# Second half of the key weights loaded ahead of the third pair of x tiles, with the orders of the head rebuilt around it

## The chip, the cores and the metric

The kernel runs on one core of a Trainium2 chip. The metric is the device time of one execution in microseconds (us); a figure for a kernel is the median of its executions. Times inside one execution count from the start of its span.

The engines are named as in the profile: PE is the tensor engine, ACT is ScalarE, DVE is VectorE, POOL is GpSimd, and SP is the engine that issues most loads.

## The reference

One transformer layer on 2048 tokens of width 448, with 16 heads of width 28: a linear attention with softmax features, then a gated unit of width 1792. Only the attention's first steps matter here.

```python
xn  = layernorm(x)                                  # over the 448 columns
q, k, v = split(xn @ wqkv)                          # 16 heads of 28
phi_k = concat(softmax(k @ w_phi), softmax(-(k @ w_phi)))   # per head
kv = einsum("bhsf,bhsd->bhfd", phi_k, v)            # summed over all tokens
...                                                 # the same features for q, division, wo
h  = x + attention
h2 = h + (sigmoid(hn @ w_gate) * (hn @ w_up)) @ w_down,   hn = layernorm(h)
```

## The kernel before

The kernel is a list of named operations, each with what it reads and writes, and one string of names for each engine that fixes the order in which that engine runs them. Waits follow from the data and the orders. The change edits these strings and hardly anything else, so the names are needed.

- The 16 tiles of x have 128 tokens each. `x1` and `x0` are loads of one tile (112 KB); `x2`, `x4` and so on are loads of a pair (224 KB), so `x2` brings tiles 2 and 3; it is the third load of x, and the texts call it the third x pair. `ld_k0` and `ld_k2` are the two halves of the key weights (196 KB each).
- `bst`, `agg`: statistics of a tile, on DVE. `ve1`, `pow1`, `nm1`, `nb1`: the scale and shift that follow from them, nearly all on POOL. `xn`: the normalized tile. `xT`: its transpose, with the copy `xTe`.
- `wT0` to `wT3` transpose the key weights on PE, `wTe` copy them out, `w2m0` multiply them by `w_phi`, and `w2e0` evict the product Wk. One product with Wk then gives k @ w_phi directly.
- `ppa0 ppb0` project tiles 0 and 1 on Wk, `vva0 vvb0` give their values; `ppa2` and the rest do the same for tiles 2 and 3. `ek` is the pair of exponentials, `ss` and `rs` the sums and reciprocals, `phi` the multiply that completes the softmax features, and `kva kvb` the product with the values.
- `warm0` to `warm9` are dummy products of zeros that keep PE busy.

The heads of the five orders, as far as the argument goes:

```python
"sp":   "x1 x0 ld_k0 x2 ld_k2 x4 x6 ld_v0 x10 ld_v2 x8 ld_q2 ld_q1 ld_q0 x12 ..."
"act":  "wphi3 wphi2 wphi1 wphi0 wTe0 wTe1 xT1e xT0e wTe2 w2e0_0 w2e0_1 w2e0_2 w2e0_3 xn3 xn4 ek0 ek1 xn5 ..."
"pe":   "warm0 warm1 warm2 wT0 wT1 xT1 warm3 xT0 warm4 warm5 wT2 w2m0_0 wT3 warm6 w2m0_1 w2m0_2 warm7 w2m0_3
         warm8 ppa0 warm9 ppb0 vva0 xT3 xT2 vvb0 ppa2 ppb2 vva2 vvb2 ..."
"dve":  "zero bd0 bst1 agg1 ve1_1 bst0 agg0 nm1_0 xn1 xn0 bst2 agg2 bst3 agg3 bst4 bst5 wTe3 agg4 agg5 bst6 ..."
"pool": "neghalf ident0 ident phipad wqpad mask0 nm1_1 pow1_1 ve1_0 pow1_0 nm1_2 mask1 ve1_2 ve1_3 pow1_3 nm1_3
         pow1_2 nb1_3 ve1_4 nm1_4 pow1_4 nb1_4 nb1_2 xn2 mask2 opad0 ve1_6 pow1_6 ve1_8 v1ones pow1_8 nb1_6 phi0
         nb1_8 xn7 phi1 phi2 phi3 ... phi8 phi9 phi11 phi12 phi13 phi14 ..."
```

The scales are worked out in groups of tiles; each group costs one `pow` on POOL, whatever its size:

```python
def rstd(ts):                       # a, b: first tile and last tile + 1; n = b - a
    ...
    op("pool", "pow1_%d" % a, lambda e: e.tensor_tensor(rst1[:, a:b], ve1[:, a:b], neghalf[:, 0:n], ALU.pow), ...)
    ...
for ts in ([0], [1], [2], [3], [4, 5], [6, 7], [8, 9, 10, 11], [12, 13, 14, 15]):
    ...
    rstd(ts)
```

And the dummies, each with its count and width:

```python
for i, (n, size) in enumerate(((9, 512), (1, 128), (1, 128), (2, 128), (1, 128), (8, 128), (4, 128), (7, 128), (9, 128), (2, 128))):
    op("pe", "warm%d" % i, warm(n, size), r=["zero"], w=[B(3)])
```

The softmax here doesn't subtract the row's maximum and nothing guards it: scores larger than these inputs give would overflow.

## Time and profile before

| of the kernel before | value |
|---|---|
| time, median of 3 runs | 205.57 us (205.4 to 205.91) |
| span of the profiled execution | 203.7 us |
| PE busy | 97% of the span |
| third x pair issued, landed | 2.17, 5.33 us |
| second half of the keys issued, landed | 2.67, 6.30 us |
| DVE turns to tile 2's statistics | 6.17 us |
| first key projection ppa0 | 10.18 us |
| first exponential ek0 | 12.12 us |
| second key projection ppa2 | 14.02 us |

A line of the timeline gives start, duration, engine, source line, operation, output and inputs with their sizes and a count; a bracket at its end holds the idle time before it and what ended that.

### The profile page before, as it was taken

Reading aid. Unit: us, or ns where it says so; the run is one execution under the profiler, and the core shown is the slowest. Engines: PE = TensorE matmul, PEld = TensorE weight load, DVE = VectorE, ACT = ScalarE, POOL = GpSimd, SP = SyncE. Lnnn points to the kernel's source line nnn. Section 1 sums busy time; section 2 is a strip of 40 time slices with the busy share of each in tenths; the row PEclk is TensorE's granted clock in tenths of the full one; section 3 lists DMA queues with packets and bytes.
Section 4 is the critical chain, followed back from the end, with each engine's and each line's share of the span. In section 5 each row is a group of like instructions: output and inputs, shape, how many; then the busy total and the mean of one; then the engine's idle time right before and its main releaser. Section 6 shows DMA issues by size and latency. Waiting matters only on the chain.

```text
span 203.7 us, 5834 instructions
## 1 busy us (share of the span) xinstructions
PE 196.7 (97%) x2474; PEld 111.6 (55%) x2474; DVE 135.9 (67%) x340; ACT 97.4 (48%) x195; POOL 57.9 (28%) x98
## 2 busy tenths in 40 slices
PE   7899999999979999999999999999999999999995
PEld 3744556655448876777444544444555555554443
DVE  5899999978799988677668967526532422262224
ACT  2889999889892544522333343323522222222220
POOL 4699999942345310400023020001400000000000
PEclk9999999999999999999999999999999999999999
DMA  6975633899522371240004511040212000004002
GB/s 163 306 139 122 77 73 66 282 295 352 141 52 55 55 100 27 55 81 0 3 0 80 119 30 28 2 77 24 56 36 60 3 0 3 0 0 138 0 0 90
DMA packets 32866, 16.25 MB, mean 80 GB/s; under 512 B 25096, under 2 KB 31944, under 8 KB 32840
## 3 DMA queue, kind: packets, MB, share of 16 engines
q1 hardware_dynamic: 32336, 15.86, 33.2%
q8 instruction: 19, 0.31, 0.7%
q10 hardware_dynamic: 504, 0.03, 0.2%
q14 instruction: 7, 0.06, 0.1%
HBM read 8.34 MB, written 1.84 MB: 50 GB/s over the span
## 4 chain that ended last, share of the span: by engine, by line
PE 89%; DVE 4%; ACT 3%; DMA 1%; issue 1%; POOL 0%; DVEq 0%
PE psum L296 82%; PE psum L852 5%; DVE st L499 2%; DMA x_sb<-in_A_x_dram 1%; ACT eq L653 1%; ACT eq L652 1%; PE psum L567 1%; ACT junk L756 1%; ACT x_sb L748 1%; PE psum L492 1%; DVE kvz L683 1%; DVE mv L500 0%; DVE b_sb L717 0%; DVE c_sb L720 0%; POOL rst L512 0%
## 5 line engine op out<-in xcount | busy, mean ns | idle before, releaser
L296 PE MATMUL psum<-xnT,wg_sb 64*128 64x512 bf16 (+1 forms) x490 | 93.3, 333 | 0.4 <-ACT eq L653 0.2
L296 PE MATMUL psum<-xnT,wu_sb 64*128 64x512 bf16 (+1 forms) x490 | 93.0, 333 | 0.0
L824 ACT ACTIVATE sg_sb<-psum 128x512 bf16<-128x512 f32 (+1 forms) x70 | 35.0, 512 | 89.6 <-PE psum L296 89.0
L825 DVE SCALAR_TENSOR_TENSOR hhT<-sg_sb,psum 128x512 bf16<-128x512 bf16 (+1 forms) x70 | 39.0, 577 | 52.5 <-ACT sg_sb L824 52.1
L296 PEld LDWEIGHTS psum<-xnT,wg_sb 64*128 64x128 bf16 x490 | 44.3, 94 | 22.9 <-DVE hhT L825 4.8
L296 PEld LDWEIGHTS psum<-xnT,wu_sb 64*128 64x128 bf16 x490 | 44.3, 94 | 13.0
L296 PE MATMUL psum<-wd_sb,hhT 64*128 64x448 bf16 x336 | 36.9, 349 | 0.0
L296 PEld LDWEIGHTS psum<-wd_sb,hhT 64*128 64x128 bf16 x336 | 17.3, 94 | 14.8 <-DVE x_sb L751 0.6
L622 POOL TENSOR_TENSOR phi<-hhT,rs 128x896 bf16<-128x896 bf16 x14 | 24.1, 1738 | 0.9 <-PE psum L296 0.8
L296 PE MATMUL psum<-Wk,xnT 64*128 64x448 bf16 x112 | 22.3, 350 | 0.2
L296 PE MATMUL psum<-wv_sb,xnT 64*128 64x448 bf16 x112 | 22.4, 351 | 0.1
L759 POOL TENSOR_SCALAR ve<-ssq 128x1 f32<-128x1 f32 x16 | 3.1, 192 | 66.1 <-ACT junk L756 65.7
L618 DVE TENSOR_REDUCE ss<-hhT 128x32 f32<-128x896 bf16 x16 | 17.0, 1062 | 0.7 <-ACT hhT L615 0.7
L296 PE MATMUL psum<-xnT,Wq 64*120 64x512 bf16 x112 | 15.0, 385 | 0.1
L729 POOL TENSOR_TENSOR o_pad<-c_sb,rden 128x448 bf16<-128x448 bf16 x10 | 9.3, 936 | 15.6 <-DVE rden L725 13.4
L296 PE MATMUL psum<-wo_o,oT 64*128 64x448 bf16 x56 | 13.2, 350 | 0.0
L296 PE MATMUL psum<-wo_e,oT 64*128 64x448 bf16 x56 | 13.1, 349 | 0.0
L756 ACT ACTIVATE junk<-x_sb,nm 128x448 bf16<-128x448 bf16 x16 | 10.6, 661 | 1.9 <-DVE nm L754 1.8
L852 PE MATMUL psum<-wd_sb,hhT 128*128 128x448 bf16 (+2 forms) x70 | 11.1, 316 | 0.0
L859 DVE SCALAR_TENSOR_TENSOR x_sb<-psum,x_sb 128x448 bf16<-128x448 f32 (+2 forms) x17 | 9.4, 591 | 2.1 <-PE psum L852 1.6
L499 DVE BATCH_NORM_STATS2 st<-x_sb 128x6 f32<-128x448 bf16 x16 | 9.4, 611 | 1.9 <-DMA x_sb<-in_A_x_dram 1.9
L296 PEld LDWEIGHTS psum<-Wk,xnT 64*128 64x128 bf16 x112 | 7.6, 94 | 5.3 <-ACT hhT L615 0.7
(87 smaller groups left out, 240.3 us busy)
## 6 DMA issues: line engine op xcount, KB each, us to landing
out_dram<-x_sb SPq DMA_DIRECT2D x15, 112.0 KB, 1.8
x_sb<-in_A_x_dram SPq DMA_DIRECT2D x7, 224.0 KB, 4.5
wd_sb<-in_B_w_down_dram SPq DMA_DIRECT2D x7, 224.0 KB, 9.3
wg_sb<-in_B_w_gate_dram SPq DMA_DIRECT2D x3, 448.0 KB, 8.2
wu_sb<-in_B_w_up_dram SPq DMA_DIRECT2D x3, 448.0 KB, 6.9
wv_sb<-in_A_wqkv_dram SPq DMA_DIRECT2D x2, 224.0 KB, 5.0
wk_sb<-in_A_wqkv_dram SPq DMA_DIRECT2D x2, 196.0 KB, 3.3
wo_e<-in_A_wo_dram SPq DMA_DIRECT2D x1, 336.0 KB, 7.9
```

The lines of the kernel that those rows point to most:

```text
L296: p = e.matmul(o, lhsT=w, rhs=r, start=st, stop=sp, tile_position=(row, 0))
L492: p = e.transpose(ps[:, kt * P:(kt + 1) * P], src, ident[:])
L499: op("dve", "bst%d" % t, lambda e: e.bn_stats(st1[:, t, :], x_sb[:, t, :]), r=[("x", t)], w=[("st1", t)])
L618: op("dve", "ss%d" % t, lambda e: e.tensor_reduce(ss[:, s, :], eks, AX.X, ALU.add), r=[("ek", s)], w=[("ss", s)])
L622: return e.tensor_tensor(phi[:, sp, :, :, :].rearrange("p b a n -> p (b a) n")[:, :, 0:56].rearrange("p b (h d) -> p b h d", h=2), eks.rea ...
L729: return e.tensor_tensor(o_pad[:, t % NO, off:off + D].rearrange("p (h d) -> p h d", h=H), c_sb[:, t % NS, :, 0:DH], rden[:, t % NS, :][:, ...
L756: op("act", "sq%d" % t, lambda e: e.activation(junk[:, t % 2, :], h_sb[:, t, :], ACT.Square, bias=nm2[:, t:t + 1], accum_out=ssq2[:, t:t + ...
L759: op("pool", "ve%d" % t, lambda e: e.tensor_scalar(ve2[:, t:t + 1], ssq2[:, t:t + 1], 1.0 / D, EPS, op0=ALU.mult, op1=ALU.add), r=[("ssq2" ...
L824: op("act", "sig" + nm, lambda e: e.activation(sg_sb[:, k, 0:N], bk(bg)[:, 0:N], ACT.Tanh, scale=0.5), r=[B(bg)], w=[("sg", k)])
L825: op("dve", "hh" + nm, lambda e: e.scalar_tensor_tensor(out=hhT[(t0 // 4) % NHH][:, ff, ns], in0=sg_sb[:, k, 0:N], scalar=1.0, in1=bk(bu)[ ...
L852: p = e.matmul(bk(b)[:, lo:hi], lhsT=hb[:, ff, TS(t)], rhs=wd_sb[:, ff, lo:hi], start=ff == 0, stop=ff == FT - 1)
L859: op("dve", "fin%d%s" % (t, nm), lambda e: e.scalar_tensor_tensor(out=h_sb[:, t, lo:hi], in0=bk(b)[:, lo:hi], scalar=0.5, in1=h_sb[:, t, l ...
```

## The change

Its intent was to load by need. The trace shows that the second keys land late (6.30 us) and that their copy wTe3 stands behind the statistics of tiles 4 and 5 on DVE. So the keys go ahead of the third x pair, and what uses them moves up on PE, ACT and DVE. POOL gets small setup steps into its waits, and three dummies go.

```diff
 sp:   x1 x0 ld_k0
-      x2 ld_k2 x4 ...  ld_q1 ld_q0 x12
+      ld_k2 x2 x4 ...  ld_q1 x12 ld_q0
 act:  wTe0 wTe1
-      xT1e xT0e wTe2 w2e0_0 ...  xn5 v1_0 v1_1
+      xT0e wTe2 xT1e w2e0_0 ...  xn5 v1_1 v1_0
 pe:
-      warm0 warm1 warm2 wT0 wT1 xT1 warm3 xT0 warm4 warm5 wT2 w2m0_0 wT3 ... ppa0 warm9 ppb0 vva0 xT3 xT2 vvb0
+      warm0 warm1 wT0 wT1 xT1 warm2 wT2 warm3 xT0 warm4 w2m0_0 wT3 ...       ppa0 warm9 xT3 ppb0 vva0 xT2 vvb0
 dve:  bst2 agg2 bst3 agg3
-      bst4 bst5 wTe3 agg4 agg5
+      wTe3 bst5 bst4 agg5 agg4                 # and small exchanges among bst7 ... agg13
 pool:
-      ident phipad ... nm1_2 mask1 ve1_2 ve1_3 ... nb1_2 xn2 mask2 opad0 ... ve1_8 v1ones pow1_8 ... phi1 phi2 phi3
+      phipad ident ... nm1_2 ve1_2 mask1 ve1_3 ... nb1_2 v1ones xn2 opad0 ... ve1_8 pow1_8 ... phi1 phi2 mask2 phi3
 dummies:
-      (9,512) 1 1 2 1 8 4 7 9 2
+      (8,512) 2 1 1 2 4 4 4 14 1               # the small ones have 128 columns
```

## The prediction

> **What bounds the kernel now.** I read the page first, for the busy shares, then the chain of waits, then the timeline of each engine over the first 20 us, because the change rewrites only orders that belong there.
>
> ```profile
> span 203.7 us, 5834 instructions
> PE 196.7 (97%) x2474; PEld 111.6 (55%) x2474; DVE 135.9 (67%) x340; ACT 97.4 (48%) x195; POOL 57.9 (28%) x98
> PE 89%; DVE 4%; ACT 3%; DMA 1%; issue 1%; POOL 0%; DVEq 0%
> ```
>
> The tensor engine (PE) is busy 97% of the span and carries 89% of the chain. Real matmuls stand nearly without a gap from about 10 us to the end: in a table by stage PE is busy 6.00 of 6.00 us from 18 to 24, from 24 to 30 and from 30 to 36, and 7.99 of 8.00 from 36 to 44. The change removes no real matmul. It can gain only by letting this block start earlier. The chain of waits (start, duration, what) shows what stands before it:
>
> ```profile
> 5.84 0.41 DVE xn_pad L528
> 6.25 0.55 DVE st L499
> 6.80 0.02 issue
> 6.82 0.18 DVE mv L500
> 7.00 0.52 DVE st L499
> 7.53 0.02 issue
> 7.55 0.18 DVE mv L500
> 7.73 1.10 DVE st L499 x2
> 8.84 0.30 DVE WkT L485
> 9.14 0.05 issue
> 9.18 0.39 PE psum L567 x4
> 9.57 0.02 issue
> 9.59 0.54 ACT Wk L485
> 10.13 0.05 issue
> 10.18 0.93 PE psum L296 x8
> ```
>
> VectorE (DVE) takes the statistics of x tiles 2 and 3, then of 4 and 5 (the x2 of 1.10 us), and only then copies the last transposed key block, WkT (wTe3). The fold into Wk (w2m0_3), its eviction by ScalarE (ACT) and the first key projection (ppa0, at 10.18) follow. So at first sight the two statistics cost ppa0 about 1.1 us, and moving wTe3 ahead of them looks like the gain. But a second chain runs beside it, on GpSimd (POOL) and ACT, and it is nearly as late:
>
> ```profile
> 10.31 0.72 POOL L512 TENSOR_TENSOR rst<-ve,neghalf 128x2 f32<-128x2 f32 x1
> 11.17 0.34 POOL L516 TENSOR_TENSOR nb<-nm,rst 128x2 f32<-128x2 f32 x2
> 11.40 0.81 ACT L525 ACTIVATE xn_pad<-x_sb,nb,rst 128x512 bf16<-128x512 bf16 x1 [0.57 <-POOL nb L516]
> 12.12 0.52 ACT L614 ACTIVATE hhT<-psum 128x448 bf16<-128x448 f32 x1
> ```
>
> ACT idles 0.57 us for nb of tiles 4 and 5, normalizes tile 4 (xn4), and only then takes the first exponential ek0, at 12.12. From there it runs ek0, ek1 with no gap until 13.94; ppa2 needs ek1's bank and starts at 14.02. PE's own work (ppa0, ppb0, vva0, two transposes, vvb0) ends at 13.98. **Two chains meet at 14.0 us**, and both must shorten for the packed block to move.
>
> **What the Trainium skill says.** "Perfetto Trace Analysis", section "Tensor Engine Instruction (MATMUL, LD_WEIGHTS)": ACT, DVE and GpSimd are strict FIFO. The trace agrees: ek0's input (ppb0) was done at 12.00, yet ek0 began only at 12.12, as xn4 before it in the queue was running out. "DMA: Bandwidth & Descriptors", section "Issuing engines are not separate DMA queues": all transfers share the same 16 DMA engines and interleave. Here the sum of a transfer's issue and its time to landing gives x1 2.9, x0 3.9, first keys 4.8, third x pair (x2) 5.4, second keys 6.3, x4 7.6 us: in issue order, so exchanging two neighbours should trade their places, not speed both. "TensorE: Matmul & The Clock Gate", section "What's actually happening": the array starts at half clock and is released after some 3.4 us of activity. The trace agrees in kind: the weight loads of the first 512-column dummies are 0.43 us apart until 3.77 and then speed up, some 2.6 us after the first matmul.
>
> **The change part by part.**
> 1. Loads exchanged. Second keys (196 KB) took 6.3 - 5.4 = 0.9 us of the queue, x2 (224 KB) 5.4 - 4.8 = 0.57 us. After: keys at 4.8 + 0.9 = 5.7, x2 at 5.7 + 0.57 = 6.27. DVE started tile 2's statistics at 6.17, right behind xn0. So x2 now lands 0.1 us too late: statistics of 2 and 3 end (agg3) at about 7.83 in place of 7.73. **Cost 0.1 us, on the second chain.**
> 2. Transposes of the second keys. wT2 ran at 7.05, behind ten dummies and xT0, although its data were there at 6.3. Now it runs at 5.75, ahead of xT0 (6.31, which waits for xn0). But ACT takes xT0e first: it can start at 6.75, when xT0 is done, and ACT idles there 0.5 us that xT1e filled before. Then at the trace's pitches: wTe2 7.25, xT1e 7.65, and the four evictions from 8.15, 0.44 apart, so the fourth ends at 8.15 + 3 x 0.44 + 0.53 = 10.0. Before it ended at 10.12.
> 3. wTe3 before the statistics of 4 and 5: at about 7.9 in place of 8.75, and w2m0_3 at about 8.3 in place of 9.18. ACT is then the limit, so of that 0.85 us only the **0.12 us** of step 2 reaches ppa0, now at about 10.05.
> 4. Dummies. 9 to 8 of 512 columns; the 34 or so small ones (1+1+2+1+8+4+7+9+2 = 35) become 33. Small ones take some 60 to 75 ns each. The large one removed frees PE at about 4.4 in place of 4.8, but wT0 waits for the first keys until 4.80 anyway: nothing gained. In the stretch after ppa0 two become one: under 0.1 us.
> 5. xT3 before ppb0: ppb0 slides by half of the 0.62 us that the two transposes took, so its end stays near 12.0. ek0 still waits for xn4, so this costs nothing.
> 6. POOL. One mask select (0.33 us) leaves the stretch before phi0, another moves one place. nb of tile 4 still follows two of the 0.57 us powers, one of 0.72 us and five small operations; it is bound by agg3. Its mask now fills the wait for agg3, which gives back about half of step 1's 0.1 us. phi0 may start 0.2 us earlier, but its first reader (kva0, 17.96) was not waiting: phi0 ended at 17.23.
> 7. x12 issued ahead of one query transpose: it lands some 1.3 us sooner, and its statistics (16.1) were not waiting. Nothing.
>
> Sum: first chain (ppa0 to vvb0) about 0.12 + 0.1 = 0.2 us shorter; second chain (agg3, nb, xn4, ek1) 0.05 to 0.1 us longer. The later one wins at 14 us: the packed block starts 0 to 0.1 us later. Time 205.57 + 0.05, less a little for repeats in which the clock is released later and the ninth large dummy would have held up wT0: I take **205.5 us**.
>
> **Rivals.**
> A. The head really shortens by the 0.85 us that wTe3 gains. For: the chain of waits puts exactly this stretch on the path. Against: the 0.57 us ACT wait for POOL and the 0.02 to 0.1 us by which both chains miss each other at 14.0. It would give 204.7.
> B. x2 lands later than worked out, at 6.6 or more, because landings vary (3.1 to 3.6 us for the same key size): everything from agg3 on slips by the excess, one for one. It would give 205.9 to 206.2.
> C. The second keys are not sooner: wT2 now stands ahead of xT0 in PE's queue and would hold up xT0, xT0e and all that ACT does after it. Landing at 6.3 would push the fourth eviction to about 10.4 and ek0 to 12.4: about 205.9.
> D. PE cools for want of dummies. PE had 8.10 busy of the first 10 us, and about three dummies in all go; the idle before wT0 grows to 0.4 us. I think it stays warm; if not, small matmuls at half speed until 10 us would cost about 1 us.
>
> **Range and chances.** The whole affair lies in some 4 us of head, and 2% is 4.1 us, so only an accident leaves the band: faster 0.01, same 0.98, slower 0.01. The three runs of before spread 0.5 us. A gives the lower and B and C the upper side: **204.9 to 206.2**.
>
> **What would show it.** Step 1: DVE waits for x_sb by about 0.1 us ahead of tile 2's statistics, near 6.3. Step 2: ACT idles about 0.5 us before its first xnT copy, and the last Wk eviction ends near 10.0. Step 3: the WkT copy on DVE stands near 7.9 and PE no longer waits for it. The core of it: xn4 still begins after an ACT wait for POOL's nb, at 11.4 to 11.5, and ppa2 at about 14.0 to 14.1. If ppa2 stands before 13.7 the second chain was not the bound and A was right; if agg3 stands after 8.0, B was. The rest of the program, from 18 us on, should be the old one, moved by the same amount; a difference arising there would make my reasoning wrong altogether.

## The result, and the profile after

| | before | changed | difference |
|---|---|---|---|
| median | 205.57 us | 205.73 us | |
| range | 205.4 to 205.91 (3 runs) | 205.44 to 205.9 (4 runs) | |
| ratio, 95% interval | | 1.0009 (0.9987 to 1.003): the same | |
| third x pair landed | 5.33 | 6.87 | +1.54 |
| second keys landed | 6.30 | 5.43 | -0.87 |
| copy wTe3 | 8.75 | 8.38 | -0.37 |
| ppa0 | 10.18 | 9.99 | -0.19 |
| xn4 | 11.40 | 12.12 | +0.72 |
| ppa2 | 14.02 | 14.72 | +0.70 |
| DVE's last addition, behind the last product | 201.41 | 201.67 | +0.26 |

A ratio is the mean time of one kernel's fast runs over that of the other's of the same rounds, so not quite the ratio of the medians. Four runs of before took part in it (median 205.49 us). A second measurement of the changed kernel (e6 below) gave 1.003 (1.0005 to 1.0056): slower by a few tenths of a per cent at most. So the first measurement alone shows no loss; what follows about the head is read from traces, one execution each.

The page of the changed kernel, its span, busy times and the chain of waits by engine:

```profile
span 204.0 us, 5831 instructions
PE 196.1 (96%) x2471; PEld 111.0 (54%) x2471; DVE 135.0 (66%) x340; ACT 97.0 (48%) x195; POOL 57.4 (28%) x98
PE 86%; ACT 4%; DVE 2%; DMA 2%; POOL 2%; issue 1%; SPq 1%; POOLq 0%
```

POOL's share of the chain has gone from 0 to 2% and that of PE from 89 to 86%: another chain now leads into the packed block. The chain of waits names it (start, duration, what):

```profile
2.67 4.21 DMA x_sb<-in_A_x_dram
...
8.88 0.57 POOL rst L512
...
11.08 0.69 POOL rst L512
...
14.72 0.95 PE psum L296 x8
```

It starts at the load of the third x pair, 4.21 us from issue to landing, and runs over DVE's statistics, POOL's powers, ACT's normalization and the exponentials to ppa2. Nothing of the key weights is left in it. First, from the timelines of the kernel before, the moments at which DVE takes tile 2's statistics and PE takes ppa2:

```profile
6.17 0.62 DVE L499 BATCH_NORM_STATS2 st<-x_sb 128x6 f32<-128x448 bf16 x1
14.02 1.73 PE L296 MATMUL psum<-Wk,xnT 64*128 64x448 bf16 x14
```

Then the changed kernel's timelines of DVE, ACT and PE (the DVE and ACT lines at 6.90 and 12.12 are links of the chain above too), with the idle time before each in brackets:

```profile
6.90 0.63 DVE L499 BATCH_NORM_STATS2 st<-x_sb 128x6 f32<-128x448 bf16 x1 [0.70 <-DMA x_sb<-in_A_x_dram]
8.38 0.36 DVE L485 COPY WkT<-psum 112x448 bf16<-112x448 bf16 x1
9.99 0.93 PE L296 MATMUL psum<-Wk,xnT 64*128 64x448 bf16 x8
12.12 0.81 ACT L525 ACTIVATE xn_pad<-x_sb,nb,rst 128x512 bf16<-128x512 bf16 x1 [0.82 <-POOL nb L516]
14.72 1.74 PE L296 MATMUL psum<-Wk,xnT 64*128 64x448 bf16 x14 [0.48 <-ACT hhT L615]
```

DVE now stands 0.70 us waiting for x. The first chain did improve: ppa0 starts 0.19 us sooner. But ACT waits 0.82 us for POOL's nb in place of 0.57, takes xn4 0.72 us later, and PE waits 0.48 us for ACT's exponentials ahead of ppa2.

So the head lost 0.7 us, yet the program lost only 0.26. The shift of the same instruction between the two traces shows where the rest went: +0.70 at ppa2, +0.57 from vva2 on (before had small waits there which the longer wait swallowed), still +0.57 at 43 us, then +0.38 until 112 us, and +0.26 from there to the end. The step at 43 us is sharp. PE's timeline of before around it, the 16 key-value products of tiles 13 and 14 (v,phi) and the query projections behind them:

```profile
42.94 0.58 PE L296 MATMUL psum<-v,phi 64*128 64x58 bf16 x16
43.36 0.84 PE L296 MATMUL psum<-xnT,Wq 64*120 64x512 bf16 x6
```

And of the changed kernel:

```profile
43.51 0.39 PE L296 MATMUL psum<-v,phi 64*128 64x58 bf16 x16
43.74 0.85 PE L296 MATMUL psum<-xnT,Wq 64*120 64x512 bf16 x6
```

From the start of the 16 products to the next group takes 43.36 - 42.94 = 0.42 us before and 43.74 - 43.51 = 0.23 us after. In the old kernel the second eight wait for tile 14's features, which POOL finishes at 43.18. In the changed kernel they don't wait. That is 0.19 us given back, and POOL's timeline of before tells why it was late there. These are the multiplies of tiles 9 and 11 (tile 10's is DVE's):

```profile
34.00 1.70 POOL L622 TENSOR_TENSOR phi<-hhT,rs 128x896 bf16<-128x896 bf16 x1 [0.39 <-PE psum L296]
36.11 2.09 POOL L622 TENSOR_TENSOR phi<-hhT,rs 128x896 bf16<-128x896 bf16 x1 [0.41 <-PE psum L296]
```

In the changed kernel, tiles 8 and 9 run back to back:

```profile
32.63 3.36 POOL L622 TENSOR_TENSOR phi<-hhT,rs 128x896 bf16<-128x896 bf16 x2
```

POOL idled 0.39 us ahead of tile 9 before, and doesn't after. The bracket puts this down to PE, but what POOL waits for there had been reached by 33.63 us. "Perfetto Trace Analysis", section "GPSIMD Engine Instruction", of the Trainium skill advises timing POOL by the spacing of starts rather than by reported durations; that spacing agrees: tiles 8 and 9 start 34.00 - 31.91 = 2.09 us apart before and 34.28 - 32.63 = 1.65 us after.

### The profile page after: what moved, and what is told of

Read it like the earlier page. It is cut to its first block, busy times and chain, and to the rows that moved or that the text cites. A ratio compares the mean times of both kernels' runs of the same rounds, so it can differ in the third digit from the quotient of the medians.

```text
span 204.0 us, 5831 instructions
## 1 busy us (share of the span) xinstructions
PE 196.1 (96%) x2471; PEld 111.0 (54%) x2471; DVE 135.0 (66%) x340; ACT 97.0 (48%) x195; POOL 57.4 (28%) x98
## 4 chain that ended last, share of the span: by engine, by line
PE 86%; ACT 4%; DVE 2%; DMA 2%; POOL 2%; issue 1%; SPq 1%; POOLq 0%
PE psum L296 80%; PE psum L852 5%; DMA x_sb<-in_A_x_dram 2%; ACT eq L653 1%; ACT eq L652 1%; SPq L395 1%; POOL rst L512 1%; ACT junk L756 1%; ACT x_sb L748 1%; DVE kvz L683 1%; PE psum L567 0%; ACT hhT L615 0%; ACT hhT L614 0%; ACT xn_pad L525 0%; POOL nm L510 0%
## 5 line engine op out<-in xcount | busy, mean ns | idle before, releaser
L622 POOL TENSOR_TENSOR phi<-hhT,rs 128x896 bf16<-128x896 bf16 x14 | 23.6, 1712 | 1.0 <-PE psum L296 1.0
```

Of the source, the lines that this page charges most:

```text
L622: return e.tensor_tensor(phi[:, sp, :, :, :].rearrange("p b a n -> p (b a) n")[:, :, 0:56].rearrange("p b (h d) -> p b h d", h=2), eks.rea ...
```

## The experiments

The theory after the result: two chains meet ahead of ppa2, and the later one sets the block. The first goes through the keys and ppa0; the second through the third x pair, POOL's powers and xn4. The change helps the first and costs the second. The first rival is that the head doesn't matter, because the change lies inside the noise. The second is that it is not the loads but the new orders on POOL or PE that cost. Each run was correct. A profile is of one execution, and it is not always a typical one: those of e1, e2, e3, e5 and e9 were the slowest of their runs, those of e6, e8 and e11 the fastest. e1 to e4 shared one chip, e5 to e8 a second, e9 to e11 a third, and e12 had a fourth.

### e1: the changed kernel with the loads in their old order

```diff
- sp: x1 x0 ld_k0 ld_k2 x2 x4     (changed kernel)
+ sp: x1 x0 ld_k0 x2 ld_k2 x4
```

> The changed kernel with one thing undone: the third x tile pair (x2) is loaded ahead of the second key half again. My theory, that the exchange of the two loads alone made tile 2's statistics 0.7 us late: x2 lands near 5.3 again, agg3 ends near 7.8 in place of 8.47, tile 4's normalization starts at 11.4 to 11.5 in place of 12.12, and ppa2 at 14.0 to 14.3 in place of 14.72; the time falls back to that of the kernel before (ratio 0.999 to 1.001). The rival, that the new orders of ACT, POOL and PE cause the delay: ppa2 stays at 14.6 or later and the ratio near 1.001 to 1.002.

Measured: 205.45 us, ratio 1.0006 (0.9992 to 1.0019). The third x pair landed at 5.79 and DVE took it without a wait, at 6.08; xn4 followed xn3 with no wait for POOL, as the theory has it. But ppa2 stood at 14.55, not at 14.0 to 14.3, and just short of the rival's 14.6. PE's and ACT's timelines say why (ppa0, then ek0):

```profile
10.62 0.93 PE L296 MATMUL psum<-Wk,xnT 64*128 64x448 bf16 x8 [0.45 <-ACT Wk L485]
12.65 0.54 ACT L614 ACTIVATE hhT<-psum 128x448 bf16<-128x448 f32 x1 [0.53 <-PE psum L296]
```

Now the first chain is the later one. The second keys landed at 6.54, wT2 ran at 6.59 and held up xT0 behind it (6.90), and ppa0 slipped to 10.62. The new orders need the early keys: without them they cost something too, which the second rival has right, but on the first chain and not on POOL. The prediction's rival C, which was wrong for the changed kernel itself, is seen here. The time does not show this cost: it is that of before, while the profiled execution took 206.05 us, and its block lost another 0.53 us between 24.8 and 26.8 us.

### e2: the kernel before with the exchange of loads alone

```diff
- sp: x1 x0 ld_k0 x2 ld_k2 x4     (kernel before)
+ sp: x1 x0 ld_k0 ld_k2 x2 x4
```

> The kernel before with only the two loads exchanged. My theory: x2 lands near 6.9, agg3 ends near 8.45, the key copy of DVE comes behind the statistics of 4 and 5 and so near 9.6, the first key projection near 11.0 and ppa2 at 14.7 to 14.9; the packed block moves by 0.6 to 0.8 us, the span by 0.3 to 0.5 us (part of it given back near 43 us). The rival, that the loads are hidden and the new orders cost it: ppa2 stays near 14.0 and the time that of before.

Measured: 205.93 us, ratio 1.0025 (1.0013 to 1.0038). The exchange alone costs, and the interval leaves out 1, so the first rival, noise, falls for the exchange: a small loss is there. For the changed kernel as a whole it falls only by e6's interval. In DVE's and PE's timelines:

```profile
7.19 0.63 DVE L499 BATCH_NORM_STATS2 st<-x_sb 128x6 f32<-128x448 bf16 x1 [1.01 <-DMA x_sb<-in_A_x_dram]
15.02 1.74 PE L296 MATMUL psum<-Wk,xnT 64*128 64x448 bf16 x14
```

The pair landed at 7.17. DVE waited 1.01 us, and ppa2 came 1.00 us later than in the profile of before, a little more than expected. The copy wTe3, still behind four statistics, slipped too, to 9.72. POOL's gap ahead of tile 9 is still there (0.39 us), and nothing was given back there, against the expectation: the shift is +0.99 at 44 us.

### e3: the kernel before with the copy wTe3 moved ahead of tiles 4 and 5

```diff
- dve: ... agg3 bst4 bst5 wTe3 agg4 agg5
+ dve: ... agg3 wTe3 bst4 bst5 agg4 agg5
```

> The kernel before with only the last key copy of DVE moved ahead of the statistics of tiles 4 and 5. Two-chains theory (the prediction's): the first key projection moves from 10.18 to about 9.9, but tile 4's normalization still waits for POOL until 11.4 and ek0 starts at 12.1, so ppa2 stays at 13.95 to 14.05 and the time is that of before within 0.1 us. The rival, that the chain of waits shown by the profile is the only one: ppa2 at 13.7 and 0.3 us off the time.

Measured: 205.67 us, ratio 1.0013 (1.0 to 1.0026). No gain: what the chain of waits of before seemed to promise (1.1 us of statistics ahead of the copy) is not there. The profile is not a clean one, though. PE's clock was released later in it (its dummies' weight loads were 0.43 us apart until 5.05 us), wT0 stood behind the dummies until 5.26, and the copy waited for PE. ppa0 stood at 10.21 and ppa2 at 14.36, both later than expected. What ppa2 waited for last was neither chain, but DVE's copies of the transposed tiles 2 and 3 (0.35 us), which came late as well. So this run shows that the copy alone gains nothing, but its trace doesn't show by how much the second chain hides it.

### e4: e3 with one power for tiles 2 and 3 on POOL

```diff
  dve as in e3
- for ts in ([0], [1], [2], [3], [4, 5], ...
+ for ts in ([0], [1], [2, 3], [4, 5], ...
- pool: pow1_0 nm1_2 mask1 ve1_2 ve1_3 pow1_3 nm1_3 pow1_2 nb1_3 ve1_4 nm1_4 pow1_4 nb1_4 nb1_2 xn2
+ pool: pow1_0 mask1 ve1_2 nm1_2 pow1_2 nb1_2 ve1_4 nm1_4 pow1_4 nb1_4 xn2
```

> As the run with the copy first, and the second chain shortened too: tiles 2 and 3 share their scale computation on POOL (one power of two columns in place of two of one), so that the nb of tile 4 comes near 10.5 in place of 11.36. Two-chains theory: now both are shorter, ek0 starts near 11.8, ppa2 at 13.6 to 13.8, and the block up to 43 us moves by 0.2 to 0.4 us; of that 0.1 to 0.3 us reach the end of the span (ratio 0.9985 to 0.9995). If something else holds ek0 or ppa2: no change against before.

Measured: 204.92 us, ratio 0.9982 (0.997 to 0.9994): faster by 0.2%. This shortens both chains. xn4 and ppa2:

```profile
11.12 0.81 ACT L525 ACTIVATE xn_pad<-x_sb,nb,rst 128x512 bf16<-128x512 bf16 x1 [0.47 <-POOL nb L516]
14.00 1.73 PE L296 MATMUL psum<-Wk,xnT 64*128 64x448 bf16 x14 [0.21 <-DVE xnT L485]
```

xn4 starts 0.28 us sooner than before, and the exponentials end at 13.70. ppa2 gains only 0.02, and not the 0.2 to 0.4 expected, for it now waits 0.21 us for DVE's copies of the transposed tiles 2 and 3, a third chain. The products behind it lost their small waits: the shift is -0.23 from there on and -0.44 at 44 us, where POOL's gap ahead of tile 9 is gone as well. So about half of the gain up to there is the head's, and the other half is the gap's (below).

### e5: the kernel before with the joint power alone

```diff
  dve as before; groups and pool as in e4
```

> The kernel before with only the joint power of tiles 2 and 3, the other half of the faster version. Two-chains theory: nb of tile 4 near 10.6, tile 4's normalization right behind tile 3's, no longer waiting for POOL; but the key copy still stands behind the statistics of 4 and 5, the first key projection stays near 10.2 and PE's own work ends near 14.0, so ppa2 stays at 13.9 to 14.1: ratio 0.999 to 1.000, clearly less gain than with both. The rival, that the gain of the faster version is all POOL's: ratio near 0.998.

Measured: 205.03 us, ratio 0.9983 (0.997 to 0.9996). It was expected to gain less than e4 and it gained as much, so the rival is right here: the gain of e4 comes with the edit of POOL, and the copy adds nothing that these runs can measure. How much of it is the shorter chain and how much the lost gap, the times don't tell. The profiled execution was the slowest of the five (205.79 us; tiles 4 and 5 landed at 8.14 and DVE waited 0.47 us for them), so its head can't be compared. Past the head it shows what e4 shows: no gap ahead of tile 9, and a shift that goes from +0.27 to +0.06 at 44 us.

### e6: the changed kernel once more

No edit.

> The changed kernel once more, for a second trace and a narrower interval. If the lateness of x2 belongs to the change and not to one execution, it lands at 6.6 to 7.2 again and ppa2 stands at 14.5 to 15.0; ratio 1.000 to 1.002.

Measured: 205.57 us, ratio 1.003 (1.0005 to 1.0056) over six runs; two of them, 206.22 and 207.31 (at a clock of 0.992), lift the mean. In the profiled execution, the fastest, the third x pair landed at 6.54 and ppa2 stood at 14.38, both a little earlier than expected. The loss of the head is thus 0.36 us here and 0.70 us in the first profile; it varies with the landing of the pair. The shift falls from +0.24 to +0.02 at 44 us, so the step of about 0.2 us repeats.

### e7: the changed kernel with the small loads of w_phi behind the x tiles

The four loads of w_phi have rows of 56 bytes and run at the same time, issued by ACT.

```diff
- act: wphi3 wphi2 wphi1 wphi0 wTe0 ...                       (changed kernel)
+ act: wTe0 ...
- sp:  x1 x0 ld_k0 ld_k2 x2 x4 x6 ld_v0 ...
+ sp:  x1 x0 ld_k0 ld_k2 x2 x4 x6 wphi3 wphi2 wphi1 wphi0 ld_v0 ...
```

> The changed kernel with the four loads of the small feature weights (56-byte rows) taken off ACT's queue and issued behind x6 on the sync engine's. They then come too late for the fold, so the time means nothing; the reading is x2's landing. If the small rows in flight from 2.5 to 6.5 us hold up x2 (sharing the same 16 engines), it lands at 6.3 or earlier in place of 6.87 and 7.17. If it is only x2's new place behind the second keys, it stays at 6.7 or later.

Measured: one run, 206.59 us, of unknown state. The third x pair landed at 6.44, between the two expectations: inconclusive on the small rows. Together with the other profiles it helps to settle the main point, though. Here are the landings in all fourteen profiles, those of before and of the changed kernel among them (median and range, us):

| | fourth load in the queue | fifth load in the queue |
|---|---|---|
| old order, 9 profiles | x pair, 5.80 (5.33 to 6.12) | second keys, 6.62 (6.15 to 7.09) |
| new order, 5 profiles | second keys, 5.54 (5.37 to 5.72) | x pair, 6.56 (6.44 to 7.17) |

The fifth load lands at the same time whichever it is. Both orders have moved the same bytes by then, so the place in the queue decides, not the tensor.

### e8: the changed kernel with the joint power

```diff
  changed kernel; groups as in e4
- pool: pow1_0 nm1_2 ve1_2 mask1 ve1_3 pow1_3 nm1_3 pow1_2 nb1_3 ve1_4 nm1_4 pow1_4 nb1_4 nb1_2 v1ones xn2
+ pool: pow1_0 mask1 ve1_2 nm1_2 pow1_2 nb1_2 ve1_4 nm1_4 pow1_4 nb1_4 v1ones xn2
```

> The changed kernel with the second chain shortened by the same joint power. If what the change loses is lost on that chain (statistics of 2 and 3, POOL, tile 4's normalization, ek0), then nb of tile 4 comes 0.4 to 0.7 us sooner than in the changed kernel, ek0 at 12.2 to 12.5, ppa2 at 14.0 to 14.3 in place of 14.72, and the time falls to 0.998 to 1.000 of before. If the chain of keys and PE is what it loses on: ppa2 stays at 14.6 and the ratio near 1.001.

Measured: 205.37 us, ratio 1.0 (0.9988 to 1.0011). ppa2 in PE's timeline:

```profile
14.11 1.74 PE L296 MATMUL psum<-Wk,xnT 64*128 64x448 bf16 x14 [0.19 <-ACT hhT L615]
```

The x pair landed at 6.56, as in e6 (6.54), and ppa2 came 0.27 us sooner than in e6, xn4 0.33 us sooner. Nothing of the first chain was touched: ppa0 stood at 10.17, and at 10.12 in e6. So in the changed kernel the second chain is the bound, which is the theory's core; both kernels lack POOL's gap, so that plays no part. The time is that of before again, though the intervals of e8 and e6 overlap a little.

### e9 and e10: what removes POOL's gap ahead of tile 9

e9 moves one of the setup steps back behind the third features, as the change does; e10 splits the first memset into three parts that write the same columns, for two more instructions at the very start of POOL's stream, where POOL has time.

```diff
e9:   (kernel before)
- pool: ... xn2 mask2 opad0 ... phi1 phi2 phi3
+ pool: ... xn2 opad0 ... phi1 phi2 mask2 phi3
e10:  (kernel before)
- op("pool", "neghalf", lambda e: e.memset(neghalf[:], -0.5), w=["neghalf"])
+ op("pool", "neghalf", lambda e: [e.memset(neghalf[:, i:i + 1 + (i == 2)], -0.5) for i in range(3)][-1], w=["neghalf"])
```

> The kernel before with one POOL instruction moved, as the change moves it: the second mask select from before phi0 to behind phi2. POOL of the kernel before stands idle for 0.39 us ahead of its tenth phi (tile 9, at 34.00), although the semaphores it waited for had come by 33.63; the changed kernel has no such gap, and its packed block gets 0.21 us back at 43 us, where kva14 waits for phi14. If the order of POOL is what removes the gap, then here too: phi14 ends near 42.8 in place of 43.18, kva15 0.2 us sooner, ratio 0.999. If the gap depends on where the instruction stands in POOL's stream (the moved one still stands ahead of tile 9): it stays at 0.35 to 0.4, and the time is that of before.

> The kernel before with two more instructions on POOL that cost nothing: the memset of the constant -0.5 is split in three, at 0.8 us, where POOL has slack until 3.8. Everything behind them stands two places later in POOL's stream. If the gap ahead of tile 9's phi belongs to a place in the stream, it is gone (or at another phi), phi14 ends near 42.8, and the time is 0.999 of before. If it belongs to what POOL waits for: it stays, and the time too.

Measured: e9 205.27 us, ratio 0.9989 (0.9968 to 1.0009); e10 205.33 us, ratio 0.9992 (0.9974 to 1.0009). Neither time differs from before. In the traces e9 keeps the gap (0.40 us) and e10 loses it. Tiles 8 and 9 on POOL in e10, then the 16 products on PE and what follows them:

```profile
32.16 3.44 POOL L622 TENSOR_TENSOR phi<-hhT,rs 128x896 bf16<-128x896 bf16 x2
43.19 0.39 PE L296 MATMUL psum<-v,phi 64*128 64x58 bf16 x16
43.42 0.85 PE L296 MATMUL psum<-xnT,Wq 64*120 64x512 bf16 x6
```

e10's head was 0.25 us late in this profile (the load x0 landed late), and the shift fell to +0.03 at 44 us. The 16 products take 43.42 - 43.19 = 0.23 us to the next group, as in the changed kernel. Two memsets that compute nothing new thus give back the same 0.2 us as the change did.

Counting POOL's records (instructions and waits) that start before tile 9's multiply gives the pattern over all kernels:

| records before tile 9 | kernels | gap, us |
|---|---|---|
| 68 | before, e2, e3, e9 | 0.37 to 0.40 |
| 65 | e4, e5, e11, e12 | 0 to 0.04 |
| 67 | e8 | 0 |
| 70 | changed, e1, e6, e7, e10 | 0 to 0.04 |

So the gap belongs to a place in POOL's stream, and shifting the stream puts another record there. In the kernels with 70, that record is tile 8's multiply, and it shows no gap. But there a delay would be hidden: in the changed kernel its waits were over 0.72 us before tile 7's multiply ended (at 31.95 and 32.67 us), whereas in the kernel before those of tile 9's were over only 0.06 us before tile 8's ended (at 33.56 and 33.62).

Why that place costs 0.4 us, no run here shows. The traces hold one hint. A DMA packet of 8 KB, of kind "instruction", on queue q14 starts 0.62 to 0.64 us after tile 9's multiply in the four kernels with 68 records (34.62 us in before). In the five with 70 it starts 0.14 to 0.44 us after tile 8's (32.77 us in the changed kernel). This points to the fetch of POOL's instructions, but the packet doesn't name its engine.

### e11 and e12: towards a version that beats both

e11 takes e4 and moves the copies of the transposed tiles 2 and 3 up, because e4's ppa2 waits for them. e12 adds one more move, which e11's trace asked for.

```diff
e11:  (e4)
- pe:   ppb0 vva0 xT3 xT2 vvb0
+ pe:   ppb0 xT3 vva0 xT2 vvb0
- dve:  agg6 agg7 agg9 bst8 agg8 agg10 xT3e xT2e
+ dve:  agg6 agg7 xT3e agg9 bst8 xT2e agg8 agg10
e12:  (e11)
- pool: pow1_0 mask1 ve1_2 ... ve1_8 v1ones pow1_8
+ pool: pow1_0 mask1 v1ones ve1_2 ... ve1_8 pow1_8
```

> The version with copy first and joint power, with the third wait at 14 us taken out too: in its trace ppa2 waited 0.21 us for DVE's copies of x tiles 2 and 3, which stand behind the statistics of 8 to 11. Here PE transposes tile 3 ahead of vva0 and DVE copies it and tile 2 ahead of two of those. Expected: ppa2 at 13.6 to 13.8 in place of 14.00, the block 0.2 to 0.3 us sooner than there, ratio 0.996 to 0.9985 of before. If POOL's phi chain and not PE sets the end of this stage: no more than 0.998.

Measured: 205.53 us, ratio 1.0001 (0.9981 to 1.0021), so both expectations were missed. ppa2 moved to 13.89, but a new wait took the place of the old one, on ACT:

```profile
14.70 0.97 ACT L485 CAST v<-psum 128x448 bf16<-128x448 f32 x2 [0.35 <-POOL v L406]
```

With the copies ahead of agg8 and agg10, POOL waited 0.55 us for the statistics. Its memset of the ones beside v came late, at 14.17, ACT's copies of v waited for it, and vva2 stood at 15.73, 0.06 us sooner than in before. This explains a part at most: the profiled execution was the fastest of the six (205.06), while the median is half a microsecond slower, and of such an execution there is no trace.

> The run with the copies early, with the wait that it made taken out: there ACT waited 0.35 us for POOL's memset of v1's ones (14.17) before it could copy v, and the second half of the pairs (vva2) started 0.2 us late. Here that memset stands at 5.9 us, where POOL is idle. Expected: ppa2 at 13.7 to 13.9, vva2 at 15.3 to 15.5 in place of 15.73, the packed block 0.3 to 0.45 us sooner than in the kernel before, 0.3 to 0.5 us at 44 us; ratio 0.9965 to 0.9985, faster than both kernels. If something else takes its place once more: no better than 0.999.

Measured: 205.05 us (205.05 to 205.56), against 205.60 for before in the same rounds; ratio 0.9978 (0.9962 to 0.9995). Its five times fall into two groups, three of 205.05 and two of 205.5. The profile fell on one of the two: x0 landed at 4.32 us, and its whole head was late, with ppa2 at 14.62. The new wait is gone in it, but the positions that were expected for the good case were not seen. By the times, e12 beats the kernel before by some 0.2%, and it keeps the loads in the old order; with the changed kernel it shared no rounds. As in e4, some of the gain is that of POOL's lost gap.

## Why the prediction was right

**The time and the verdict** were right: 205.5 predicted, 205.73 measured, inside 204.9 to 206.2 and the same within 2%. The frame was right too. Two chains meet at 14 us, and the later one decides. ppa2 did not follow ppa0, which came sooner, but xn4, which came later; e8 shows it by shortening the second chain alone. Rival A, 0.85 us from the copy, is out: the changed kernel has the copy early and the block late, and e3 moves the copy alone for no gain. Rival D is out: the eight transposes wT0 and wT1 take 0.62 us and ppa0 0.93 in both profiles, so PE did not slow down. (The mean granted clock of 1.00 would not show it; see the last section.)

**Terms 2 and 3, the first chain**, were sized well: the last eviction of Wk ended at 9.93 (10.0 predicted) and ppa0 stood at 9.99 (10.05). The copy wTe3 came at 8.38 rather than 7.9, behind the late statistics, and still cost nothing, since ACT was the limit as predicted. (Term 2 puts ten dummies ahead of wT2; the lines have nine behind xT0 and two before it.)

**Term 1, the landing of the x pair, was mis-sized.** It allowed 0.1 us on the second chain; the profile showed 0.70 us of waiting and agg3 0.74 us later, at 8.47. So xn4 stood at 12.12 and not at 11.4 to 11.5, and ppa2 at 14.72 and not at 14.0 to 14.1. By the prediction's own sign (agg3 after 8.0) this is Rival B, a loss of 0.70 us at ppa2; B's time of 205.9 to 206.2 did not come. The arithmetic was nearly sound for one profile: the two loads together would end at 6.27, as they had ended at 6.30 (the pair had landed at 5.33 and not 5.4, so the keys took 0.97 us and not 0.9). But this was a single sample, and an early one. In nine profiles of the old order the fifth load landed at 6.15 to 7.09, with a median of 6.62, and in five of the new order at 6.56. Against DVE's 6.17 the usual cost is therefore an estimated 0.4 us (6.56 - 6.17), and the profiled 0.7 was an unlucky sample on top; DVE's waits in the five were 0.23 to 1.01 us, with a median of 0.45. e2 shows that the exchange by itself costs 0.25% of the time.

**Term 5** held that xT3 ahead of ppb0 costs nothing. ppb0 in fact slipped by 0.43 us, to 11.69, since xT3 waited for a late xn3. It did not matter, as ek0 waited for xn4 until 12.85. The conclusion held, and the size did not.

**Term 4** held: wT0 ran at 4.68, as soon as the first keys had landed at 4.64, and the missing dummies left no idle time that reached the end. **Term 6** hoped that POOL's setup steps would give time back in the head. They could not, because POOL was waiting for the late statistics: from the end of agg3 to tile 3's power POOL took 0.41 us in both profiles (7.73 to 8.14, 8.47 to 8.88), so the moved mask gave back nothing, and the first features began at 16.0 us, not 0.2 us sooner than the 15.5 of before but 0.4 later. Term 7 was not tested by itself; x12 landed 0.77 us sooner (12.13 against 12.90) and not 1.3.

**The rest being the old one, moved by the same amount, failed.** The prediction said that a difference arising past 18 us would make its reasoning wrong altogether; that was too strong, but a difference did arise. The block's shift fell from 0.57 to 0.38 us at 43 us because the shifted stream of POOL lost a 0.39 us gap ahead of tile 9's multiply; e10 reproduces this in the old kernel with two memsets, without the rest of the change. Another 0.1 us went at one place too, ahead of the first products with `wo`. They read a tile that a DMA transposes: in before its transpose landed at 112.29, 4.16 us after its issue, and the products started at 112.38. In the changed kernel it took 2.49 us and nothing waited. It took 2.48 to 2.49 us in six of the fourteen profiles and 4.00 to 4.57 in eight, with the changed orders and without, so this part is no proven effect of the change.

How the gap reached PE can be followed. With it, POOL's multiply of tile 9 ran until 35.70 and overlapped DVE's of tile 10, which took 1.43 us in place of the 1.08 of e10 (the line of before, then that of e10); that in turn overlapped POOL's of tile 11, which took 2.09 in place of 1.70.

```profile
35.21 1.43 DVE L622 TENSOR_TENSOR phi<-hhT,rs 128x896 bf16<-128x896 bf16 x1
35.46 1.08 DVE L622 TENSOR_TENSOR phi<-hhT,rs 128x896 bf16<-128x896 bf16 x1
```

"SBUF — State Buffer", section "Who interferes with whom", of the Trainium skill says that a DVE instruction with two SBUF inputs contends with a POOL instruction that reads SBUF, and that the ports they share are an exclusive lock. The trace agrees in kind. The two overlaps are 35.70 - 35.21 = 0.49 and 36.64 - 36.11 = 0.53 us, and the stretches 0.35 and 0.39, each the overlap less 0.14. In the changed kernel an overlap of 0.20 stretched tile 10's multiply by 0.07, and in e10 one of 0.18 stretched tile 11's by 0.04: the overlap less 0.13 and 0.14. (The spacing of POOL's starts gives the same stretches. For DVE only the slope is measured: its base, the 1.08 of e10, has itself an overlap of 0.13 with tile 9's multiply.)

So the time was right partly because two errors nearly cancelled: the head lost 0.6 us more than predicted, and the shorter waits at vva2, the lost gap and the early transpose gave back 0.44 of it. None of these was foreseen, and that they came close to the loss was luck.

**What stays open:** the cause of POOL's gap; whether the small rows of w_phi slow the x pair; why the transpose takes 2.5 or 4 us; and the head of e12 in its fast runs, of which there is no trace.

## What to carry to other kernels

When two loads are exchanged, the second of the pair lands when both used to have landed; ask which consumer has the slack for that, and take the landing from several profiles, because a single one was off by 0.3 us here. Where several chains meet, shortening the one that the profile names may move nothing: here the copy on the named chain gained nothing, and one power on POOL in place of two gained 0.2%, of which the traces give about half to the head and the rest to waits far behind it. Compare the same instructions across two traces all the way to the end, for a reordering can also change waits far behind the part that was reordered.

## What the Trainium skill lacked or had wrong

- No page has a figure for POOL idling at one place of its instruction stream with what it waits for already reached; the page on the runtime, "Runtime: NRT & Kernel Launch", treats the fetch of instructions and gives no duration for a stall of this kind. Here it is 0.37 to 0.40 us ahead of one multiply when 68 records stood before it, and 0.04 or less with 65, 67 or 70 (e10 removes it with two memsets). That it is a fetch is not shown.
- "SBUF — State Buffer" calls the shared ports an exclusive lock. The traces agree, with a correction worth having: the recorded stretch was 0.13 to 0.14 us less than the recorded overlap in the four cases measured above (0.49, 0.53, 0.20 and 0.18 us of overlap; the two of POOL, 0.53 and 0.18, have a base without overlap), so the overlap of 0.18 us cost POOL 0.04.
- "DMA: Bandwidth & Descriptors" says that transfers interleave on the same engines. It has no figure for how far one landing varies between executions: the fifth load landed at 6.15 to 7.09 us over nine profiles of the same load order, one each of nine kernels on several chips.
- "TensorE: Matmul & The Clock Gate" puts the release of the clock at around 4 us of activity, give or take 0.5, and says that it varies from run to run. It does vary, and by more: with the first dummy at 1.24 us, the wide dummies' weight loads stayed 0.43 us apart until 3.77 us in the profile of before. In e3 they did so until the wide dummies had ended, at 5.05, and the eight transposes behind them still took 0.95 us in place of 0.62. The trace's own record of the full clock starts at 3.98 us in before and at 6.58 in e3, so 2.7 and 5.3 us after the first dummy. The mean granted clock of the profile did not show the difference: it reads 1.00 for both executions.
